# Small inputs as plain rows, and the output projection in longer runs, half of it loaded ahead of the last V tiles

## The chip, the cores and the metric

The kernel runs on one core of one Trainium2 chip. The metric is the device time in microseconds (us). All executions quoted here are fast (none is more than 1.5% above the fastest of its kernel), and their spread is given. A profiled execution is described by its span, from the first to the last instruction. The span is about 1.7 us shorter than the device time of the same execution.

A ratio below is the mean time of one kernel's fast runs over the mean time of the other's fast runs of the same rounds. It is therefore not quite the ratio of the medians that stand beside it. The interval is 95%. "Faster" and "slower" as verdicts need 2%.

## The reference

One decode step for four sequences (B = 4, one token each, D = 1024) mixes an attention block and an MLP block with a gate. H = 32 heads, Sk = 8192 cached positions, Dh = 128, F = 3584, all bf16. Cut to what matters:

```python
g = sigmoid((x * gate_w).sum(-1))
# A: attention over the cache
q = (x @ wq).reshape(B, 1, H, Dh)
p = softmax(q . k_cache * Dh**-0.5)
a = (p . v_cache).reshape(B, 1, H * Dh) @ wo
# B: MLP, scaled by sigmoid(x @ w_r)
y = (silu(x @ w_gate) * (x @ w_up)) @ w_down
b = x + y * sigmoid(x @ w_r)
return g * a + (1 - g) * b
```

The K and V caches are 268 MB each and each byte is used once. With the weights the kernel reads 576 MB.

## The kernel before

All large inputs go through a ring of five buffers of 128 x 32 KB (4 MB each), loaded by one queue (SP) in a fixed order. A "piece" is one such load: two heads of K or V of one sequence, or a part of a weight matrix. A piece is loaded as soon as the ring's oldest buffer has been used. There are 64 K pieces and 64 V pieces. V runs four pieces behind K, so the last four V pieces come after the last K. I call them V60 to V63.

The small inputs come in on another queue (ACT), already transposed by the access pattern, in runs of 16 bytes:

```python
    with nc.allow_non_contiguous_dma(reason="16-byte runs of x, w_r and gate_w"):
        nc.scalar.dma_start(out=xT[:], in_=x2.rearrange("b (c t) -> c b t", t=DT))
        nc.scalar.dma_start(out=wrg[:, 0, :], in_=B_w_r.rearrange("(c t) -> c t", t=DT))
        nc.scalar.dma_start(out=wrg[:, 1, :], in_=gate_w.rearrange("(c t) -> c t", t=DT))
    nc.scalar.dma_start(out=x_sb[:], in_=x2)
```

The program starts with the gates, which need `wrg` and `xT`, and then with q, which needs wq and `xT`:

```python
    gates()
    wq_piece(0)
    wq_piece(TW)
    q_done()
    # ... [cut: the list of MLP pieces put between the first K and V pieces]
    for u in range(NT + LAG):
        if u < NT:
            k_piece(u)
        if u >= LAG:
            v_piece(u - LAG)
        # ... [cut]
```

One V piece is 32 matmuls of 128x8 by 128x512, a copy by ScalarE, and four small fp32 matmuls that transpose the result back (the profile counts them as eight). After every fourth piece VectorE writes the normalized result of eight heads to `OT`:

```python
        o_sb = osp.tile([NM, 4 * Dh], F32, name="o_sb")
        nc.scalar.copy(out=o_sb[:], in_=o_ps[:])
        def finish():
            # ... [cut]
            for q in range(4):
                nc.tensor.matmul(oT[:, HT * t:HT * t + HT], lhsT=o_sb[:, q * Dh:(q + 1) * Dh],
                                 rhs=ident[0:NM, q:NM:4], start=(q == 0), stop=(q == 3))
            if t == GT - 1:
                # ... [cut: OT = oT * gate / row sum]
```

The output projection comes last, in pieces of 16, 12, 3 and 1 heads. Each run in memory is one row of wo, 2 KB:

```python
    wov = A_wo.rearrange("(h d) n -> d h n", d=P)
    def wo_piece(h0, nh):
        w = slot()[:, :nh * D].rearrange("p (h n) -> p h n", h=nh)
        nc.sync.dma_start(out=w, in_=wov[:, h0:h0 + nh, :])
        for h in range(nh):
            for n in range(NH):
                mm_acc(acc[:, n * NB:(n + 1) * NB], OT[:, h0 + h, :], w[:, h, n * NB:(n + 1) * NB])
```

Of the kernel before, what the change touches and what calls it, by code (L numbers as in the profile page):

```python
# [9 lines left out]
BF = mybir.dt.bfloat16  # L10
F32 = mybir.dt.float32
# [8 lines left out]
def kernel(  # L20
# [22 lines left out]
    nc = tc.nc  # L43
    P = 128
    Bn, Sq, D = A_x.shape
    _, H, Sk, Dh = A_k_cache.shape
    F = B_w_gate.shape[1]
    DT = D // P
# [4 lines left out]
    GH = GT * HT  # L53
# [3 lines left out]
    NT = Bn * H // HT  # L57
    LAG = 4
    FR = 4
    FG = F // (P * FR)  # L60
    NB = 512
    NH = D // NB
    RING = JR * Dh
# [3 lines left out]
    x2 = A_x.rearrange("b s d -> (b s) d")  # L67
    out2 = out.rearrange("b s d -> (b s) d")

    const = ctx.enter_context(tc.tile_pool(name="const", bufs=1))  # L70
# [8 lines left out]
    ops = ctx.enter_context(tc.tile_pool(name="ops", bufs=2, space=PSUM))  # L79
    o2p = ctx.enter_context(tc.tile_pool(name="o2p", bufs=1, space=PSUM))  # L80

    def slot():
        return ring.tile([P, RING], BF, name="piece", tag="piece")


    xT = const.tile([P, Bn, DT], BF)
    wrg = const.tile([P, 2, DT], BF)
    x_sb = const.tile([Bn, D], BF)
    with nc.allow_non_contiguous_dma(reason="16-byte runs of x, w_r and gate_w"):
        nc.scalar.dma_start(out=xT[:], in_=x2.rearrange("b (c t) -> c b t", t=DT))  # L90
        nc.scalar.dma_start(out=wrg[:, 0, :], in_=B_w_r.rearrange("(c t) -> c t", t=DT))
        nc.scalar.dma_start(out=wrg[:, 1, :], in_=gate_w.rearrange("(c t) -> c t", t=DT))
    nc.scalar.dma_start(out=x_sb[:], in_=x2)


    shr = shrp.tile([P, 512], F32)
    nc.vector.memset(shr[:], 0.0)
    ident = const.tile([P, P], F32)
    make_identity(nc, ident[:])
    R = const.tile([P, 4, P], BF)  # L100
    nc.gpsimd.memset(R[:], 0.0)
    for he in range(4):
# [21 lines left out]
    qT = const.tile([P, H, Bn], BF)  # L124
    qa = const.tile([P, 4, H, Bn], BF)
    OT = const.tile([P, H, Bn], BF)
    hT = const.tile([P, FG, FR, Bn], BF)
    sgb = const.tile([P, 2, Bn], F32)
    c12 = const.tile([P, 2, Bn], F32)
# [3 lines left out]
    gu_ps = shr[:, o0:o0 + 2 * FT * Bn].rearrange("p (w g r b) -> p w g r b", w=2, g=FG, r=FR); o0 += 2 * FT * Bn  # L133
# [3 lines left out]
    acc = accp.tile([Bn, D], F32)  # L137

    def mm_acc(out_ap, lhsT, rhs, start=False):
        nc.tensor.matmul(out_ap, lhsT=lhsT, rhs=rhs, start=start, stop=True, skip_group_check=True)  # L140


    def gates():
        wrep = ttp.tile([P, 2, DT, P], BF, name="wrep", tag="T")
        for i in range(2):
            nc.vector.tensor_copy(out=wrep[:, i, :, :], in_=wrg[:, i, :].unsqueeze(2).to_broadcast([P, DT, P]))  # L146
            for t in range(DT):
                mm_acc(rg_ps[:, i, :], wrep[:, i, t, :], xT[:, :, t])
        nc.scalar.activation(out=sgb[:], in_=rg_ps, func=ACT.Sigmoid)
        nc.vector.tensor_scalar(out=c12[:, 0, :], in0=sgb[:, 1, :], scalar1=-1.0, scalar2=1.0, op0=ALU.mult, op1=ALU.add)  # L150
        nc.vector.tensor_tensor(out=c12[:, 1, :], in0=c12[:, 0, :], in1=sgb[:, 0, :], op=ALU.mult)
        xf = ttp.tile([Bn, D], F32, name="xf", tag="T")
        nc.vector.tensor_copy(out=xf[:], in_=x_sb[:])
        dg = const.tile([Bn, Bn], F32)
        nc.vector.tensor_tensor(out=dg[:], in0=ident[0:Bn, 0:Bn], in1=c12[0:Bn, 0, :], op=ALU.mult)
        for n in range(NH):
            mm_acc(acc[:, n * NB:(n + 1) * NB], dg[:], xf[:, n * NB:(n + 1) * NB], start=True)
# [3 lines left out]
    wgv = B_w_gate.rearrange("(c t) f -> c t f", t=DT)  # L161
    wuv = B_w_up.rearrange("(c t) f -> c t f", t=DT)
    wdv = B_w_down.rearrange("(g f r) n -> f g r n", f=P, r=FR)
    wov = A_wo.rearrange("(h d) n -> d h n", d=P)
    TW = 4

    def wq_piece(t0):
        w = slot()[:, :TW * H * Dh].rearrange("p (t h d) -> p t h d", t=TW, h=H)
        nc.sync.dma_start(out=w.rearrange("p t h d -> p t (h d)"), in_=wqv[:, t0:t0 + TW, :])
        for t in range(TW):  # L170
            for h in range(H):
                mm_acc(q_ps[:, h, :], w[:, t, h, :], xT[:, :, t0 + t])

    def q_done():
        nc.vector.tensor_copy(out=qT[:], in_=q_ps)
# [6 lines left out]
    def gu_piece(view, w_i, t0):  # L182
        w = slot()[:, :TW * F].rearrange("p (t g f r) -> p t g f r", t=TW, g=FG, r=FR)
        nc.sync.dma_start(out=w.rearrange("p t g f r -> p t (g f r)"), in_=view[:, t0:t0 + TW, :])
        for t in range(TW):
            for g in range(FG):
                for r in range(FR):
                    mm_acc(gu_ps[:, w_i, g, r, :], w[:, t, g, :, r], xT[:, :, t0 + t])

    def h_done():  # L190
        g_sb = stat.tile([P, FT, Bn], F32, tag="g_sb", bufs=1)
        fl = lambda ap: ap.rearrange("p g r b -> p (g r) b")
        nc.scalar.activation(out=g_sb[:], in_=fl(gu_ps[:, 0]), func=ACT.Silu)
        nc.vector.tensor_tensor(out=g_sb[:], in0=g_sb[:], in1=fl(gu_ps[:, 1]), op=ALU.mult)
        nc.vector.tensor_tensor(out=fl(hT[:]), in0=g_sb[:],
                                in1=c12[:, 1:2, :].to_broadcast([P, FT, Bn]), op=ALU.mult)

    def wd_piece(g0, ng):
        w = slot()[:, :ng * FR * D].rearrange("p (g r n) -> p g r n", g=ng, r=FR)
        nc.sync.dma_start(out=w.rearrange("p g r n -> p g (r n)"),  # L200
                          in_=wdv[:, g0:g0 + ng].rearrange("f g r n -> f g (r n)"))
        for g in range(ng):
            for r in range(FR):
                for n in range(NH):
                    mm_acc(acc[:, n * NB:(n + 1) * NB], hT[:, g0 + g, r, :], w[:, g, r, n * NB:(n + 1) * NB])

    def wo_piece(h0, nh):
        w = slot()[:, :nh * D].rearrange("p (h n) -> p h n", h=nh)
        nc.sync.dma_start(out=w, in_=wov[:, h0:h0 + nh, :])
        for h in range(nh):  # L210
            for n in range(NH):
                mm_acc(acc[:, n * NB:(n + 1) * NB], OT[:, h0 + h, :], w[:, h, n * NB:(n + 1) * NB])


    S_ps = {}
# [4 lines left out]
    def flush():  # L220
        while pending:
            pending.pop(0)()
# [4 lines left out]
    def kv_view(cache, u):  # L227
        b, h0 = heads(u)
        return cache[b, h0:h0 + HT].rearrange("h (r j) d -> (h r) (j d)", j=JR)
# [63 lines left out]
    def v_piece(u):  # L293
        b, h0 = heads(u)
        g, t = divmod(u, GT)
        B_ = PB[g % 2]
        vn = slot()
        nc.sync.dma_start(out=vn[:], in_=kv_view(A_v_cache, u))
        o_ps = ops.tile([NM, 4 * Dh], F32, name="o_ps")
        n = 0  # L300
        for jc in range(JC):
            for uq in range(4):
                j0 = 16 * jc + 4 * uq
                nc.tensor.matmul(o_ps[:, :], lhsT=B_[:, JC * t + jc, uq].rearrange("p s j -> p (s j)"),  # L304
                                 rhs=vn[:, j0 * Dh:(j0 + 4) * Dh], start=(n == 0), stop=(n == JR // 4 - 1))
                n += 1
                if n == 8:
                    flush()
# [4 lines that stand above are left out]
            if t == 0:  # L313
                oT_t[g] = o2p.tile([P, GH], F32, name="oT")
            oT = oT_t[g]
# [4 lines that stand above are left out]
                oT_t.pop(g)  # L320
                hg = h0 + HT - GH
                nc.vector.scalar_tensor_tensor(out=OT[:, hg:hg + GH, b], in0=oT[:, :], scalar=sgb[:, 1, b:b + 1],  # L322
                                               in1=rinv_t.pop(g)[:], op0=ALU.mult, op1=ALU.mult)
        pending.append(finish)
# [5 lines left out]
    q_done()  # L330
    side = [lambda: gu_piece(wgv, 0, 0), lambda: gu_piece(wgv, 0, TW), lambda: gu_piece(wuv, 1, 0),
            lambda: (gu_piece(wuv, 1, TW), h_done()), lambda: wd_piece(0, 4), lambda: wd_piece(4, FG - 4)]
    for u in range(NT + LAG):
        if u < NT:
            k_piece(u)
        if u >= LAG:
            v_piece(u - LAG)
        if side:
            side.pop(0)()
    for s in side:  # L340
        s()
    flush()
    h0 = 0
    for nh in (16, 12, 3, 1):
        if h0 + nh <= H:
            wo_piece(h0, nh)
            h0 += nh
    assert h0 == H
    res = const.tile([Bn, D], BF)
    nc.vector.tensor_copy(out=res[:, 0:NB], in_=acc[:, 0:NB])  # L350
    nc.sync.dma_start(out=out2[:, 0:NB], in_=res[:, 0:NB])
# [32 lines left out]
```

## Time and profile before

| | before |
|---|---|
| device time, median of 4 runs | 1361.61 us (1361.4 to 1361.76) |
| span of the profiled run | 1359.9 us |
| bytes moved | 576.49 MB |
| first use of a wq piece | 48.4 us |
| first transpose of the last K piece | 1280.6 us |
| last output matmul ends | 1356.5 us |

The overview page has a line with the rate of the transfers in 40 equal slices of the span (34 us each), in GB/s:

```profile
GB/s 398 389 431 430 428 430 431 432 430 430 431 431 430 430 430 431 432 431 431 430 431 431 431 431 431 431 431 431 431 432 431 431 430 430 430 430 431 430 425 237
```

36 of the 40 slices are at 428 to 432. At 431 GB/s the bytes need 1337.5 us, and the span is 22 us longer. All of that is in the first two slices and the last two. As long as the middle stays at that rate, faster compute there cannot show in the time.

*The front.* The first lines of the chain of waits, in order of time (start in us, duration in us, what the time went to):

```profile
1.29 41.08 DMA wrg<-in_B_w_r_dram
42.37 0.02 issue
42.39 1.31 DVE wrep L146 x2
...
48.42 5.51 PE shr L140 x203
```

For 41 us TensorE and VectorE wait for w_r, a vector of 2 KB. The transfers run meanwhile, since the ring can be filled without anyone using it. But only four of its five buffers were being filled. SP, which issues these loads, waited 37.3 us for xT, one of the small inputs, before it issued the fifth:

```profile
40.05 0.33 SPq L242 DMA_DIRECT2D piece<-in_A_k_cache_dram  x1
```

For 41 us TensorE and VectorE wait for w_r, a vector of 2 KB. The ring can be filled meanwhile, but the sixth load needed a free buffer, so it had to wait until the first wq piece had been used (51.96 us). The transfers run dry. The windows show GB/s (the columns are the window and its length, busy us and number of instructions of PE, PE weight loads, DVE, ACT, POOL, then the granted TensorE clock, the DMA share and GB/s):

```profile
40.00:45.00 5.00, 0.91 (x17) 0.67 (x18) 2.45 (x9) 0.18 (x1) 0.00 (x0) 1.00 0.90 314
50.00:55.00 5.00, 4.82 (x182) 4.76 (x179) 0.00 (x0) 0.00 (x0) 0.00 (x0) 1.00 0.84 312
55.00:60.00 5.00, 1.62 (x30) 1.12 (x28) 3.63 (x4) 1.28 (x1) 1.56 (x8) 1.00 0.93 387
```

Against 431 GB/s this is a loss of 1.35 + 1.4 + 0.5 = 3.3 us. The queue table gives packets, MB, and share of the 16 engines' time; q1 is SP's queue, q10 is ACT's:

```profile
q1 hardware_dynamic: 24392, 575.68, 98.9%
q10 hardware_dynamic: 832, 0.02, 0.0%
```

So the small loads cost no DMA time to speak of, yet take 41 us to land. The same view for the stretch from 5 to 40 us shows why: in these 35 us both queues moved the same number of packets (469 of SP's have 28 or 32 KB, 501 of ACT's have 16 bytes, and the rest of both have 4 bytes).

```profile
q1 hardware_dynamic: 517, 14.86, 99.5%
q10 hardware_dynamic: 517, 0.01, 0.8%
```

*The tail.* The end of the chain of waits:

```profile
1292.97 7.01 PE o_ps L304 x32
...
1300.01 40.80 DMA piece<-in_A_wo_dram
...
1340.85 15.67 PE acc L140 x64
...
1356.55 0.57 ACT res L352
```

The long DMA link is the time in the queue of the first wo piece, behind the rest of V61, V62 and V63 (322 packets of 32 KB were still to come at 1300.0). TensorE's own list shows that it had to wait 1.91 us for V63.

```profile
1330.09 8.75 PE L304 MATMUL o_ps<-piece,PB_129 128*8 128x512 bf16 x32 [1.91 <-DMA piece<-in_A_v_cache_dram]
```

32 such matmuls take 7.07 us at full clock; here they took 8.75 us, with the clock granted in that window at 0.66. The Trainium skill ("TensorE: Matmul & The Clock Gate", Part 1) says that idleness halves TensorE's clock, in windows of 3.4 us; the trace agrees: its clock records have half clock from 1330.66 to 1334.07 us, and again from 1340.90 to 1344.31, where the 64 output matmuls took 15.67 us instead of 14.1 (twice 7.07).

### The profile page before, as it was taken

What the parts mean: (1) busy time and instruction counts of PE and PEld (TensorE: products, weight loads), DVE (VectorE), ACT (ScalarE), POOL (GpSimd) and SP (SyncE); (2) the same over time, 40 slices, a digit from 0 to 9 for tenths busy, and PEclk for the clock granted to TensorE, in tenths of its full rate; (3) what the DMA queues carried; (4) which work ended last, traced back from release to release, by engine and by line L of the source; (5) the groups of instructions that cost most, each with busy time, mean ns of one, the idle gap of its engine ahead of it and who ended that gap; (6) DMA issues with size and microseconds to landing.
All of it is one profiled execution on the core that took longest, in us unless ns stands there. A gap on an engine that the chain in (4) does not pass through costs nothing.

```text
span 1359.9 us, 12458 instructions
## 1 busy us (share of the span) xinstructions
PE 1115.9 (82%) x5456; PEld 481.1 (35%) x5456; DVE 621.3 (46%) x399; ACT 70.9 (5%) x118; POOL 84.2 (6%) x322
## 2 busy tenths in 40 slices
PE   0595998888888888878798888978988888888897
PEld 0352333333333333333333333333333333333343
DVE  0364355444544545365445535554554445445500
ACT  0000000000000000000000000000000000000010
POOL 1000000000000000000000000000000000000000
PEclk9987998999898989989999998989989998989998
DMA  9999999999999999999999999999999999999996
GB/s 398 389 431 430 428 430 431 432 430 430 431 431 430 430 430 431 432 431 431 430 431 431 431 431 431 431 431 431 431 432 431 431 430 430 430 430 431 430 425 237
DMA packets 25278, 576.49 MB, mean 424 GB/s; under 512 B 3068, under 2 KB 3076, under 8 KB 7176
## 3 DMA queue, kind: packets, MB, share of 16 engines
q1 hardware_dynamic: 24392, 575.68, 98.9%
q8 instruction: 42, 0.69, 0.2%
q10 hardware_dynamic: 832, 0.02, 0.0%
q14 instruction: 12, 0.10, 0.0%
HBM read 575.69 MB, written 0.01 MB: 423 GB/s over the span
## 4 chain that ended last, share of the span: by engine, by line
DMA 44%; PE 39%; DVE 11%; issue 4%; ACT 1%; POOL 0%; ACTq 0%; DVEq 0%
DMA piece<-in_A_k_cache_dram 38%; PE S_ps L252 17%; PE o_ps L304 17%; DVE T L245 11%; DMA wrg<-in_B_w_r_dram 3%; DMA piece<-in_A_wo_dram 3%; PE acc L140 2%; PE shr L140 2%; PE oT L317 1%; ACT o_sb L310 1%; DVE OT L322 0%; DVE wrep L146 0%; POOL PB_128 L282 0%; ACT PTs L275 0%; DVE PT L277 0%
## 5 line engine op out<-in xcount | busy, mean ns | idle before, releaser
L245 DVE STREAM_TRANSPOSE T<-piece 128x2048 uint32<-128x2048 uint32 x256 | 577.3, 2291 | 487.9 <-DMA piece<-in_A_k_cache_dram 390.0
L252 PE MATMUL S_ps<-T,Z_126 128*128 128x512 bf16 x1024 | 281.8, 429 | 92.9 <-DVE T L245 92.6
L252 PE MATMUL S_ps<-T,Z_127 128*128 128x512 bf16 x1024 | 264.0, 408 | 54.5 <-DVE T L245 54.5
L304 PE MATMUL o_ps<-piece,PB_129 128*8 128x512 bf16 x1024 | 227.9, 381 | 2.0 <-DMA piece<-in_A_v_cache_dram 1.9
L304 PE MATMUL o_ps<-piece,PB_128 128*8 128x512 bf16 x1024 | 226.2, 379 | 0.0
L252 PEld LDWEIGHTS <-Z_126 128*128 128x128 bf16 x1024 | 108.9, 106 | 253.2 <-issue 168.4
L252 PEld LDWEIGHTS <-Z_127 128*128 128x128 bf16 x1024 | 103.5, 102 | 201.3 <-issue 107.7
L304 PEld LDWEIGHTS <-PB_129 128*8 128x8 bf16 x1024 | 86.9, 87 | 139.0 <-issue 16.3
L304 PEld LDWEIGHTS <-PB_128 128*8 128x8 bf16 x1024 | 86.4, 87 | 137.3 <-issue 13.6
L317 PE MATMUL oT<-ident,o_sb 8*128 8x2 f32 x512 | 67.1, 249 | 46.3 <-ACT o_sb L310 46.3
L317 PEld LDWEIGHTS oT<-ident,o_sb 8*128 8x128 f32 x512 | 61.6, 186 | 78.5 <-ACT o_sb L310 78.5
L310 ACT COPY o_sb<-o_ps 8x512 f32<-8x512 f32 x64 | 36.7, 574 | 923.0 <-PE o_ps L304 923.0
L236 POOL COPY Z_126<-qa 32x4 bf16<-32x4 bf16 x128 | 24.9, 195 | 567.8 <-PE S_ps L252 523.0
L236 POOL COPY Z_127<-qa 32x4 bf16<-32x4 bf16 x128 | 24.9, 194 | 549.6 <-PE S_ps L252 544.1
L322 DVE SCALAR_TENSOR_TENSOR OT<-oT,sgb,rinv 128x8 bf16<-128x8 f32 x16 | 3.8, 236 | 89.9 <-PE oT L317 89.9
L140 PE MATMUL shr<-xT,wrep 128*128 128x4 bf16 x16 | 0.8, 171 | 43.4 <-DVE wrep L146 43.4
L140 PEld LDWEIGHTS <-piece 128*128 128x128 bf16 x704 | 22.5, 112 | 2.9 <-issue 2.0
L140 PE MATMUL shr<-xT,piece 128*128 128x4 bf16 x704 | 22.6, 171 | 0.2 <-issue 0.2
L275 ACT ACTIVATE PTs<-S_ps,negm 128x512 bf16<-128x512 f32 x16 | 11.0, 687 | 224.0 <-DVE negm L272 224.0
L146 DVE COPY wrep<-wrg 128x1024 bf16<-128x1024 bf16 x2 | 1.3, 690 | 40.9 <-DMA wrg<-in_B_w_r_dram 40.9
L277 DVE STREAM_TRANSPOSE PT<-PTs 128x512 bf16<-128x512 bf16 x16 | 11.4, 712 | 13.5 <-ACT PTs L275 13.5
L140 PEld LDWEIGHTS <-wrep 128*128 128x128 bf16 x16 | 0.6, 106 | 43.4 <-DVE wrep L146 43.4
(85 smaller groups left out, 133.7 us busy)
## 6 DMA issues: line engine op xcount, KB each, us to landing
piece<-in_A_k_cache_dram SPq DMA_DIRECT2D x64, 4096.0 KB, 38.0
piece<-in_A_v_cache_dram SPq DMA_DIRECT2D x64, 4096.0 KB, 37.9
piece<-in_A_wq_dram SPq DMA_DIRECT2D x2, 4096.0 KB, 22.6
piece<-in_B_w_gate_dram SPq DMA_DIRECT2D x2, 3584.0 KB, 40.0
piece<-in_B_w_up_dram SPq DMA_DIRECT2D x2, 3584.0 KB, 17.3
piece<-in_B_w_down_dram SPq DMA_DIRECT2D x1, 4096.0 KB
piece<-in_A_wo_dram SPq DMA_DIRECT2D x1, 4096.0 KB
piece<-in_B_w_down_dram SPq DMA_DIRECT2D x1, 3072.0 KB, 24.3
```

The costliest lines, as they stand in the source:

```text
L140: nc.tensor.matmul(out_ap, lhsT=lhsT, rhs=rhs, start=start, stop=True, skip_group_check=True)
L146: nc.vector.tensor_copy(out=wrep[:, i, :, :], in_=wrg[:, i, :].unsqueeze(2).to_broadcast([P, DT, P]))
L236: nc.gpsimd.tensor_copy(out=Z[32 * a:32 * a + 32, :, 31 + 32 * a:32 + 32 * a], in_=qa[32 * a:32 * a + 32, :, h0 + a // QH, b:b + 1])
L245: nc.vector.transpose(out=T[:].rearrange("p j h i e -> p (j h i e)").bitcast(U32), in_=kn[:, c * CJ * Dh:(c + 1) * CJ * Dh].bitcast(U32))
L252: nc.tensor.matmul(sps[:, :], lhsT=Z[:, he, s:s + P], rhs=T[:, 16 * jl:16 * jl + 16, half, :, e], start=(t == 0 and jc == 0 and he == 0), ...
L275: nc.scalar.activation(out=PTs[:], in_=sps[:], func=ACT.Exp, bias=negm[:, 0:1], scale=scale, accum_out=rs[:, 0:1])
L277: nc.vector.transpose(out=PT[:].rearrange("p j i -> p (j i)"), in_=PTs[:])
L304: nc.tensor.matmul(o_ps[:, :], lhsT=B_[:, JC * t + jc, uq].rearrange("p s j -> p (s j)"), rhs=vn[:, j0 * Dh:(j0 + 4) * Dh], start=(n == 0) ...
L310: nc.scalar.copy(out=o_sb[:], in_=o_ps[:])
L317: nc.tensor.matmul(oT[:, HT * t:HT * t + HT], lhsT=o_sb[:, q * Dh:(q + 1) * Dh], rhs=ident[0:NM, q:NM:4], start=(q == 0), stop=(q == 3))
L322: nc.vector.scalar_tensor_tensor(out=OT[:, hg:hg + GH, b], in0=oT[:, :], scalar=sgb[:, 1, b:b + 1], in1=rinv_t.pop(g)[:], op0=ALU.mult, op ...
```

## The change

The intent at the front is to load x, w_r and gate_w as six plain rows of 2 KB and to transpose them on TensorE. The intent at the tail is threefold. wo is read in runs of 8 KB (four consecutive rows per partition), which makes it necessary to permute the attention output the same way (`o_rows`, 16 small matmuls with a strided identity). The first 4 MB of wo are loaded ahead of V61 and used before it. The last V comes in four transfers of 1 MB. The core of the diff:

```diff
-        nc.scalar.dma_start(out=xT[:], in_=x2.rearrange("b (c t) -> c b t", t=DT))
-        nc.scalar.dma_start(out=wrg[:, 0, :], in_=B_w_r.rearrange("(c t) -> c t", t=DT))
-        nc.scalar.dma_start(out=wrg[:, 1, :], in_=gate_w.rearrange("(c t) -> c t", t=DT))
-    nc.scalar.dma_start(out=x_sb[:], in_=x2)
+    x6 = const.tile([NX, D], BF)
+    nc.scalar.dma_start(out=x6[0:Bn], in_=x2)
+    nc.scalar.dma_start(out=x6[Bn:Bn + 1], in_=B_w_r.rearrange("(o n) -> o n", o=1))
+    nc.scalar.dma_start(out=x6[Bn + 1:Bn + 2], in_=gate_w.rearrange("(o n) -> o n", o=1))
 # ... [cut]
+    for t in range(DT):
+        nc.tensor.transpose(out=xw_ps[:, t, :], in_=x6[:, t:D:DT], identity=identb[0:NX, 0:NX])
 # ... [cut: uses of xT; and below, o_rows]
-    wov = A_wo.rearrange("(h d) n -> d h n", d=P)
+    wov = A_wo.rearrange("(g p r) n -> p g r n", p=P, r=FR)
+    def wo_piece(g0, g1, r0=0, r1=FR):
+        ng, nr = g1 - g0, r1 - r0
+        w = slot()[:, :ng * nr * D].rearrange("p (g r n) -> p g r n", g=ng, r=nr)
+        nc.sync.dma_start(out=w.rearrange("p g r n -> p g (r n)"),
+                          in_=wov[:, g0:g1, r0:r1].rearrange("p g r n -> p g (r n)"))
 # ... [cut: returns a function that does the matmuls, on LT instead of OT]
-        nc.sync.dma_start(out=vn[:], in_=kv_view(A_v_cache, u))
+        cut = 4 if u == NT - 1 else 1
+        for c in range(cut):
+            lo, hi = c * RING // cut, (c + 1) * RING // cut
+            nc.sync.dma_start(out=vn[:, lo:hi], in_=vv[:, lo:hi])
 # ... [cut]
+    GE = NWB - GH // WB          # 6 of 8 groups of 512 rows
+    GS = GE // 2 + 1             # 4
     for u in range(NT + LAG):
         if u < NT:
             k_piece(u)
+        if u == NT + 1:
+            flush()
+            o_rows(0, GE)
+            wo_piece(0, GS)()
         if u >= LAG:
             v_piece(u - LAG)
-    for nh in (16, 12, 3, 1):
-        # ... [cut]
+    early = wo_piece(GS, GE)
+    late = [wo_piece(GE, NWB - 1), wo_piece(NWB - 1, NWB, 0, FR - 1), wo_piece(NWB - 1, NWB, FR - 1, FR)]
     flush()
+    early()
+    o_rows(GE, NWB)
+    for use in late:
+        use()
```

More of the change, by code (lines that the diff above doesn't have):

```diff
@@ L83, in slot @@
         return ring.tile([P, RING], BF, name="piece", tag="piece")
-    xT = const.tile([P, Bn, DT], BF)
-    wrg = const.tile([P, 2, DT], BF)
-    x_sb = const.tile([Bn, D], BF)
-    with nc.allow_non_contiguous_dma(reason="16-byte runs of x, w_r and gate_w"):
-        nc.scalar.dma_start(out=xT[:], in_=x2.rearrange("b (c t) -> c b t", t=DT))
-        nc.scalar.dma_start(out=wrg[:, 0, :], in_=B_w_r.rearrange("(c t) -> c t", t=DT))
-        nc.scalar.dma_start(out=wrg[:, 1, :], in_=gate_w.rearrange("(c t) -> c t", t=DT))
-    nc.scalar.dma_start(out=x_sb[:], in_=x2)
+    NX = Bn + 2
+    x6 = const.tile([NX, D], BF)
+    nc.scalar.dma_start(out=x6[0:Bn], in_=x2)
+    nc.scalar.dma_start(out=x6[Bn:Bn + 1], in_=B_w_r.rearrange("(o n) -> o n", o=1))
+    nc.scalar.dma_start(out=x6[Bn + 1:Bn + 2], in_=gate_w.rearrange("(o n) -> o n", o=1))
     shr = shrp.tile([P, 512], F32)
@@ L99 @@
     make_identity(nc, ident[:])
+    identb = const.tile([P, P], BF)
+    nc.vector.tensor_copy(out=identb[:], in_=ident[:])
+    xw_ps = o2p.tile([P, DT, NX], BF, name="xw", tag="oT")
+    for t in range(DT):
+        nc.tensor.transpose(out=xw_ps[:, t, :], in_=x6[:, t:D:DT], identity=identb[0:NX, 0:NX])
+    xw = const.tile([P, DT, NX], BF)
+    nc.vector.tensor_copy(out=xw[:], in_=xw_ps[:])
+    xT = [xw[:, t, 0:Bn] for t in range(DT)]
     R = const.tile([P, 4, P], BF)
@@ L126 @@
     OT = const.tile([P, H, Bn], BF)
+    LT = const.tile([P, FR, H // FR, Bn], BF)
     hT = const.tile([P, FG, FR, Bn], BF)
@@ L145, in gates @@
         for i in range(2):
-            nc.vector.tensor_copy(out=wrep[:, i, :, :], in_=wrg[:, i, :].unsqueeze(2).to_broadcast([P, DT, P]))
+            nc.vector.tensor_copy(out=wrep[:, i, :, :], in_=xw[:, :, Bn + i:Bn + i + 1].to_broadcast([P, DT, P]))
             for t in range(DT):
-                mm_acc(rg_ps[:, i, :], wrep[:, i, t, :], xT[:, :, t])
+                mm_acc(rg_ps[:, i, :], wrep[:, i, t, :], xT[t])
         nc.scalar.activation(out=sgb[:], in_=rg_ps, func=ACT.Sigmoid)
@@ L152, in gates @@
         xf = ttp.tile([Bn, D], F32, name="xf", tag="T")
-        nc.vector.tensor_copy(out=xf[:], in_=x_sb[:])
+        nc.vector.tensor_copy(out=xf[:], in_=x6[0:Bn])
         dg = const.tile([Bn, Bn], F32)
@@ L171, in wq_piece @@
             for h in range(H):
-                mm_acc(q_ps[:, h, :], w[:, t, h, :], xT[:, :, t0 + t])
+                mm_acc(q_ps[:, h, :], w[:, t, h, :], xT[t0 + t])
     def q_done():
@@ L187, in gu_piece @@
                 for r in range(FR):
-                    mm_acc(gu_ps[:, w_i, g, r, :], w[:, t, g, :, r], xT[:, :, t0 + t])
+                    mm_acc(gu_ps[:, w_i, g, r, :], w[:, t, g, :, r], xT[t0 + t])
     def h_done():
@@ L205, in wd_piece, with o_rows, use @@
                     mm_acc(acc[:, n * NB:(n + 1) * NB], hT[:, g0 + g, r, :], w[:, g, r, n * NB:(n + 1) * NB])
-    def wo_piece(h0, nh):
-        w = slot()[:, :nh * D].rearrange("p (h n) -> p h n", h=nh)
-        nc.sync.dma_start(out=w, in_=wov[:, h0:h0 + nh, :])
-        for h in range(nh):
-            for n in range(NH):
-                mm_acc(acc[:, n * NB:(n + 1) * NB], OT[:, h0 + h, :], w[:, h, n * NB:(n + 1) * NB])
+    WB = P * FR // Dh
+    NWB = H // WB
+    def o_rows(g0, g1):
+        n = g1 - g0
+        lp = ops.tile([P, FR, n, Bn], F32, name="o_ps")
+        for k in range(WB):
+            for r in range(FR):
+                nc.tensor.matmul(lp[32 * k:32 * k + 32, r], lhsT=identb[:, r:P:FR],
+                                 rhs=OT[:, WB * g0 + k:WB * g1:WB, :], start=True, stop=True, skip_group_check=True)
+        nc.vector.tensor_copy(out=LT[:, :, g0:g1, :], in_=lp[:])
+    def wo_piece(g0, g1, r0=0, r1=FR):
[3 more added lines that the diff above has]
+                          in_=wov[:, g0:g1, r0:r1].rearrange("p g r n -> p g (r n)"))
+        def use():
+            for g in range(ng):
+                for r in range(nr):
+                    for n in range(NH):
+                        mm_acc(acc[:, n * NB:(n + 1) * NB], LT[:, r0 + r, g0 + g, :], w[:, g, r, n * NB:(n + 1) * NB])
+        return use
     S_ps = {}
@@ L297, in v_piece @@
         vn = slot()
-        nc.sync.dma_start(out=vn[:], in_=kv_view(A_v_cache, u))
+        vv = kv_view(A_v_cache, u)
+        cut = 4 if u == NT - 1 else 1
+        for c in range(cut):
+            lo, hi = c * RING // cut, (c + 1) * RING // cut
+            nc.sync.dma_start(out=vn[:, lo:hi], in_=vv[:, lo:hi])
         o_ps = ops.tile([NM, 4 * Dh], F32, name="o_ps")
@@ L339 @@
             side.pop(0)()
-    for s in side:
-        s()
+    early = wo_piece(GS, GE)
+    late = [wo_piece(GE, NWB - 1), wo_piece(NWB - 1, NWB, 0, FR - 1), wo_piece(NWB - 1, NWB, FR - 1, FR)]
     flush()
-    h0 = 0
-    for nh in (16, 12, 3, 1):
-        if h0 + nh <= H:
-            wo_piece(h0, nh)
-            h0 += nh
-    assert h0 == H
+    early()
+    o_rows(GE, NWB)
+    for use in late:
+        use()
     res = const.tile([Bn, D], BF)
```

## The prediction

> **What bounds the kernel now.** The transfers. The 40-slice page shows 428 to 432 GB/s in 36 of 40 slices; 576.49 MB at 431 GB/s is 1337.5 us of a 1359.9 us span, so 22 us are lost, at the two ends. The groups agree: VectorE waits 390 us for K pieces.
>
> *Front.* The chain starts with 41.1 us of DMA for w_r. TensorE cannot use wq until x and w_r are there, so none of the ring's five 4 MB slots comes free. The windows show 314 GB/s in 40:45, 312 in 50:55, 387 in 55:60: against 431 a loss of 1.35 + 1.4 + 0.5 = 3.3 us. The queue table gives the cause: 832 packets on the ACT queue, 0.0% of the engines' time, yet 41 us. The Trainium skill ("DMA: Bandwidth & Descriptors", Queues, rings and completion order) says each DMA engine alternates between queue rows packet by packet; 16-byte packets behind 28 to 32 KB ones fit that.
>
> *Tail.* The last V lands near 1330 (TensorE idles 1.9 us for it), its matmuls end at 1338.9, the transpose back at 1340.6, 64 output matmuls take 15.7 us to 1356.5; copy, store and end 3.4 us. The last wo transfer is done by 1351: TensorE ends this stage.
>
> **The change.** Front: 6 rows of 2 KB replace 768 16-byte runs; they should land within 10 us. Added: an identity cast, 8 small transposes, one copy. The identity is only ready at 13.9 us (timeline), so wq is used from about 16 us instead of 48, before the ring drains at 47: the 3.3 us stall goes, plus perhaps 0.2 us of packet cost. Gain 3.5 us, all critical, carried through the DMA-bound middle: last K at 1277 instead of 1280.5.
>
> Tail: half of wo (4 MB, 9.7 us) moves ahead of V61. DMA lands, at 9.73 us per 4 MB: V59 1286.5, V60 1296, wo 1306, V61 1316, V62 1325.5, V63 1335 in quarters, rest of wo by 1345. From V62's landing TensorE has 7.07 (V62) + 1.05 (transpose back) + 7.07 (V63) + 0.65 (ScalarE copy) + 1.05 + 0.35 (OT), 16 permuting matmuls (estimate 1.2), 32 output matmuls at 0.22 (7.1): 25.5 us, end 1351. So it is TensorE-bound from V62 on. Before, V63's landing to the last matmul took 26.5 us; now 16 plus the 9.7 of wo put in front: about 1 us gained. The 8 KB runs save 1 us per 4 MB (10.7 against 9.7), but where nothing waits any more.
>
> Clock: the windows show 0.66 granted in 1330:1335 and 1340:1345, after idle stretches. "TensorE: Matmul & The Clock Gate" (Part 1) says idleness halves the clock in 3.4 us windows; each costs some 1.8 us here. The new tail may have one too.
>
> **Prediction.** Last matmul 1351, +3.4 = 1354.4 span, +1.7 from span to time = 1356.1, plus 0.9 for half a throttle window: 1357.0 us, 8 in 10 between 1353 and 1360. Faster by over 2% 0.01, within 2% 0.98, slower 0.01.
>
> **Signs.** Right: no 41 us DMA link at the start; slices 1 and 2 near 430 after the first 3 us; first output matmuls near 1307; the final chain TensorE from V62 or V63 on, late wo landed before use. Wrong: a new DMA dip before 60 us; the last wo piece as last releaser; V61 to V63 waiting for slots.
>
> **What would make it wrong.** Small rows landing late after all; output or permuting matmuls slower than 0.22 and 0.08 us; throttle windows falling differently; the early wo making TensorE late at V61.

## The result, and the profile after

| | before | changed |
|---|---|---|
| device time, median of 4 runs | 1361.61 us (1361.4 to 1361.76) | 1357.22 us (1356.14 to 1358.29) |
| ratio of the fast runs | | 0.9968 (0.9951 to 0.9985) |
| span of the profiled run | 1359.9 us | 1354.7 us |
| first use of a wq piece | 48.4 us | 23.5 us |
| first transpose of the last K piece | 1280.6 us | 1276.6 us |
| last output matmul ends | 1356.5 us | 1351.7 us |

The changed kernel is 4.4 us faster by the medians, 0.3%. The spans differ by 5.2 us, because the profiled run was one of the two quicker of the four. Of these 5.2 us, 4.0 were there when the last K piece was transposed. Only 0.8 us were gained from there to the last output matmul, and 0.4 us behind it. Counted in the packet records of the two traces, any number of bytes between 22 and 545 MB was reached about 3.5 us earlier (3.1 to 3.8) in the changed kernel. Some 1.3 to 1.75 us of that are there at 17 to 20 MB, in the fifth load, and the rest comes with the sixth.

The rates of the slices, page of the changed kernel. The second slice went from 389 to 428; the middle is as it was:

```profile
GB/s 404 428 432 427 427 432 430 433 431 429 430 431 430 433 431 430 429 432 431 430 433 431 430 431 430 429 432 432 431 433 431 432 428 429 431 432 433 432 422 257
```

ACT's queue in the queue table has 20 packets instead of 832:

```profile
q10 hardware_dynamic: 20, 0.02, 0.0%
```

SP issues the fifth load at 2.84 us instead of 40.05. The front of the chain of waits no longer has a DMA link. It begins with 11.54 us in which POOL waited for nothing that the profile shows, and then POOL builds constants, among them the identity (13.56 us in the kernel before, so this is not new, only hidden no longer). Then follow a VectorE cast of 2.12 us (0.67 in the kernel before; why, was not looked into), the fp32 matmuls of the residual, and the first use of wq at 23.57 us:

```profile
1.73 11.54 issue
13.27 0.28 POOL ident masks.py:199
...
17.34 2.12 DVE xf L159
...
20.00 3.57 PE acc L146 x4
23.57 5.29 PE shr L146 x195
```

The windows in which the transfers had run dry (the same columns as before) now show 455, 392 and 454 GB/s:

```profile
40.00:45.00 5.00, 4.25 (x19) 1.77 (x18) 4.39 (x2) 0.00 (x0) 0.00 (x0) 1.00 1.05 455
50.00:55.00 5.00, 0.51 (x4) 0.18 (x2) 2.83 (x2) 0.00 (x0) 0.00 (x0) 0.54 0.92 392
55.00:60.00 5.00, 4.46 (x16) 1.66 (x15) 3.92 (x3) 0.00 (x0) 0.00 (x0) 0.78 1.05 454
```

The mean of the three is 434, and the slice that holds them (34 to 68 us) is at 428 instead of 389, so the 392 is at most a small part of the old loss. The end of the chain of waits:

```profile
1275.09 42.07 DMA piece<-in_A_v_cache_dram
1317.16 0.04 issue
1317.20 8.51 PE o_ps L333 x32
...
1326.42 1.05 PE oT L346 x8
1327.47 8.73 PE o_ps L333 x40
1336.19 0.98 PE oT L346 x8
1337.17 5.29 PE o_ps L333 x24
...
1343.16 1.06 PE oT L346 x8
...
1344.25 0.25 DVE OT L351
...
1344.88 6.87 PE acc L146 x31
```

From V61's landing at 1317.16 us there is no DMA in the chain any more. TensorE works through V61, V62 and V63 (32 + 40 + 24 matmuls; the 40 are V62 and the first quarter of V63), the transposes back, and the last 32 output matmuls. TensorE's own list shows the price of the early piece ahead of V61:

```profile
1307.48 7.07 PE L146 MATMUL acc<-piece,LT 128*4 128x512 bf16 x32 [0.99 <-DMA piece<-in_A_wo_dram]
1317.20 8.50 PE L333 MATMUL o_ps<-piece,PB_139 128*8 128x512 bf16 x32 [2.65 <-DMA piece<-in_A_v_cache_dram]
```

It takes TensorE 7.07 us to use 4 MB of wo, and the transfers 9.7 us to bring them. The difference is a wait of 2.65 us before V61, and the clock then is halved for a part of V61 (8.50 instead of 7.07 us).

### The profile page after: what moved, and what is told of

It reads as the page before. It is cut to its first block, busy times and chain, and to the rows that moved or that the text cites. A ratio compares the mean times of both kernels' runs of the same rounds, so it can differ in the third digit from the quotient of the medians.

```text
span 1354.7 us, 12547 instructions
## 1 busy us (share of the span) xinstructions
PE 1119.6 (83%) x5496; PEld 483.1 (36%) x5496; DVE 624.2 (46%) x403; ACT 71.0 (5%) x118; POOL 85.2 (6%) x322
## 4 chain that ended last, share of the span: by engine, by line
DMA 48%; PE 33%; DVE 11%; issue 7%; ACT 1%; POOL 0%; DVEq 0%; ACTq 0%; POOLq 0%
DMA piece<-in_A_k_cache_dram 45%; PE o_ps L333 17%; PE S_ps L277 13%; DVE T L270 10%; DMA piece<-in_A_v_cache_dram 3%; PE acc L146 1%; PE oT L346 1%; PE shr L146 1%; ACT o_sb L339 1%; DVE OT L351 0%; DVE xf L159 0%; POOL Z_137 L127 0%; POOL R L109 0%; POOL PB_138 L307 0%; DVEq L270 0%
## 5 line engine op out<-in xcount | busy, mean ns | idle before, releaser
L333 PEld LDWEIGHTS <-PB_138 128*8 128x8 bf16 x1024 | 86.4, 87 | 137.3 <-issue 13.6
L146 PE MATMUL shr<-xw,piece 128*128 128x4 bf16 x704 | 22.6, 170 | 1.7 <-issue 1.7
L146 PE MATMUL acc<-piece,LT 128*4 128x512 bf16 x64 | 14.1, 379 | 1.0 <-DMA piece<-in_A_wo_dram 1.0
L313 DVE RECIPROCAL rinv<-tot 128x8 f32<-128x8 f32 x16 | 3.2, 203 | 25.3 <-POOL tot L311 25.3
L146 PE MATMUL acc<-piece,hT 128*4 128x512 bf16 x56 | 12.4, 379 | 0.0
## 6 DMA issues: line engine op xcount, KB each, us to landing
piece<-in_A_wq_dram SPq DMA_DIRECT2D x2, 4096.0 KB, 13.1
```

What stands on the lines that cost most here:

```text
L146: nc.tensor.matmul(out_ap, lhsT=lhsT, rhs=rhs, start=start, stop=True, skip_group_check=True)
L313: nc.vector.reciprocal(out=rinv[:], in_=tot[:])
L333: nc.tensor.matmul(o_ps[:, :], lhsT=B_[:, JC * t + jc, uq].rearrange("p s j -> p (s j)"), rhs=vn[:, j0 * Dh:(j0 + 4) * Dh], start=(n == 0) ...
```

## The experiments

Theory A: the front brings the gain, because in a kernel bound by transfers a stall of the transfers is never made up; in the tail TensorE has a fixed sum of work behind the last V pieces, and neither run length nor the early half removes any of it. Theory B: the tail brings the gain. (The expectations also name a theory C or D, or a rival, for a single run.) Twelve kernels ran, all correct, each for five rounds beside the kernel before. The medians of before in the three groups of runs were 1361.32, 1361.60 and 1361.65 us.

| run | median us (range) | ratio to before (95%) |
|---|---|---|
| front_only | 1357.32 (1356.93 to 1358.68) | 0.9973 (0.9960 to 0.9985) |
| tail_only | 1361.97 (1360.47 to 1363.41) | 1.0006 (0.9994 to 1.0019) |
| wo_all_late | 1357.68 (1356.81 to 1358.17) | 0.9973 (0.9961 to 0.9986) |
| small_behind_wq | 1357.61 (1357.61 to 1359.41) | 0.9977 (0.9963 to 0.9991) |
| no_cut | 1357.60 (1356.91 to 1358.55) | 0.9970 (0.9956 to 0.9984) |
| more_early | 1358.46 (1358.38 to 1361.22) | 0.9983 (0.9970 to 0.9995) |
| late_split | 1352.66 (1352.46 to 1353.31) | 0.9933 (0.9921 to 0.9946) |
| keep_warm | 1357.43 (1355.67 to 1357.77) | 0.9964 (0.9951 to 0.9976) |
| late_split_2k | 1353.99 (1353.80 to 1354.32) | 0.9941 (0.9929 to 0.9954) |
| simple_both | 1354.61 (1354.52 to 1354.74) | 0.9945 (0.9933 to 0.9958) |
| keep_warm_2 | 1357.31 (1355.66 to 1357.94) | 0.9962 (0.9950 to 0.9975) |
| after_again | 1357.69 (1355.76 to 1359.12) | 0.9967 (0.9953 to 0.9980) |

### front_only: the front alone

Edit: the changed kernel with the old tail put back.

```diff
-    wov = A_wo.rearrange("(g p r) n -> p g r n", p=P, r=FR)
+    wov = A_wo.rearrange("(h d) n -> d h n", d=P)
 # ... o_rows, early half and the cut of the last V removed; 16, 12, 3, 1 heads at the end
```

Expected:

> The new loads of x, w_r and gate_w with the old tail (2 KB runs of wo, all of it after the last V, last V in one transfer). Theory A, front first: the ended stall moves every later transfer 3.5 to 3.9 us forward and the old tail follows unchanged, so 1357.9 us (1357.3 to 1358.5), last K in the trace near 1276.7 instead of 1280.5. Theory B, tail first: a stall in the first 60 us is made up in the 1250 us that follow, or the old tail waits for something else, and this kernel stays above 1360.5 us.

Measured: 1357.32 us, 4.0 us below before by the medians. The last K landed at 1276.5 us in the chain of waits. Theory A holds for the front, and within the spread this is all of the gain of the full change (1357.22 and, again, 1357.69 us).

### tail_only: the tail alone

Edit: the kernel before with the new tail (and the bf16 identity that it needs).

```diff
+    identb = const.tile([P, P], BF)
+    nc.vector.tensor_copy(out=identb[:], in_=ident[:])
-    wov = A_wo.rearrange("(h d) n -> d h n", d=P)
+    wov = A_wo.rearrange("(g p r) n -> p g r n", p=P, r=FR)
 # ... o_rows, early half and the cut of the last V as in the change
```

Expected:

> The old loads with the new tail. Theory A: last K as before at 1280.5 us, the tail from there on shorter by 0.5 to 2 us, so 1360.6 us (1359.6 to 1361.3). Theory B, the early half of wo and its 8 KB runs bring most of the gain: 1358.5 us or less.

Measured: 1361.97 us, ratio 1.0006 with an interval from 0.9994 to 1.0019. The gain of about 1 us that theory A gave it did not appear (the median is 0.7 us above A's range), and the gain of 3 us that theory B gave it is excluded. In the profiled run two half-clock stretches fell into the tail: 40 matmuls of V took 10.13 us instead of 8.8, and the last 31 output matmuls 8.55 instead of 6.87. They don't explain the missing gain, for the tail of the kernel before has two as well. Without them, the old tail took 26.5 - 3.2 = 23.3 us from V63's landing (1330.05) to the last output matmul, and the new one 27.4 - 3.0 = 24.4 us from V62's landing at nearly the same time (1330.30). At equal clock the new tail is no shorter.

### small_behind_wq: old 16-byte runs, other queue

Edit, against the kernel before: the four small loads are issued on the queue of the weights, directly behind the first wq piece.

```diff
+    wq0 = slot()[:, :4 * H * Dh].rearrange("p (t h d) -> p t h d", t=4, h=H)
+    nc.sync.dma_start(out=wq0.rearrange("p t h d -> p t (h d)"),
+                      in_=A_wq.rearrange("(c t) n -> c t n", t=DT)[:, 0:4, :])
-        nc.scalar.dma_start(out=xT[:], in_=x2.rearrange("b (c t) -> c b t", t=DT))
+        nc.sync.dma_start(out=xT[:], in_=x2.rearrange("b (c t) -> c b t", t=DT))
 # ... the same for w_r, gate_w and x_sb; wq_piece(0) uses wq0
```

Expected:

> The kernel before, 16-byte runs kept, but the four small loads are issued on the same queue as the weights, directly behind the first wq piece. Theory A (each small packet had to let a 28 to 32 KB packet of the other queue pass): on one queue they run one after the other and land at 12 to 16 us instead of 41, and the time is 1358.2 us (1357.5 to 1358.9), as with plain rows. Rival C (the 16-byte runs are slow in themselves): w_r lands after 25 us or later, or the transfers behind them are held up by as much, and at least 1360.5 us.

Measured: 1357.61 us. The list of DMA issues (queue, count, KB, us from issue to landing) of the kernel before:

```profile
wrg<-in_B_w_r_dram ACTq DMA_DIRECT2D x1, 2.0 KB, 41.1
wrg<-in_gate_w_dram ACTq DMA_DIRECT2D x1, 2.0 KB, 40.7
```

and of small_behind_wq:

```profile
wrg<-in_B_w_r_dram SPq DMA_DIRECT2D x1, 2.0 KB, 13.1
wrg<-in_gate_w_dram SPq DMA_DIRECT2D x1, 2.0 KB, 12.7
```

The same 16-byte runs land in 13.1 us, most of which is the 4 MB of wq ahead of them: in the packet records all 768 start between 12.0 and 14.1 us. Rival C, that the short runs are slow in themselves, falls. The 41 us came from standing in a queue of their own beside a queue of large packets. The Trainium skill ("DMA: Bandwidth & Descriptors", Queues, rings and completion order) says that each DMA engine takes turns between the queues that have work, one packet at a time. The trace of the kernel before agrees: 517 packets of each queue from 5 to 40 us, so a turn cost a small packet 1.08 us (35 us on 16 engines for 517 packets). The plain rows and the transposes of the change are therefore one cure of two, and the other one needs no new instruction.

### wo_all_late: nothing of wo ahead of a V

Edit, against the changed kernel:

```diff
-            wo_piece(0, GS)()
-    early = wo_piece(GS, GE)
+    early = [wo_piece(0, GS), wo_piece(GS, GE)]
 # ... and both are used behind the last V
```

Expected:

> The changed kernel, but the first 4 MB of wo are loaded after the last V, with the same 8 KB runs; nothing of wo stands ahead of a V. Theory A: TensorE's work after the last K is the same and only its waits move (about 3 us for the first wo piece instead of 3.7 us before V61), so the last output matmul ends near 1350 to 1351.5 in the trace and the time is 1355 to 1357.5 us, no slower than the changed kernel. Theory B: half the output matmuls go back behind the last V, 32 times 0.22 us, so 1361 us or more.

Measured: 1357.68 us, 0.2 us above the range given, and the same as the changed kernel (1357.22 and 1357.69). Moving half of wo ahead of V61 is worth nothing that can be measured: theory B does not hold. Theory A's time was nearly met, but not its trace, where the last output matmul was to end by 1351.5 us; in the profiled run it ended at 1353.3. TensorE's list shows what it waits for now:

```profile
1336.67 16.65 PE L146 MATMUL acc<-piece,LT 128*4 128x512 bf16 x64 [2.51 <-DMA piece<-in_A_wo_dram]
```

It waits 2.51 us for the first wo piece of 4 MB, and then runs 64 matmuls in 16.65 us, at half clock for a part of them, where 64 at full clock take 14.1 (2 x 7.07).

### late_split: the same in transfers of 1 MB

Edit, against wo_all_late:

```diff
-        nc.sync.dma_start(out=w.rearrange("p g r n -> p g (r n)"),
-                          in_=wov[:, g0:g1, r0:r1].rearrange("p g r n -> p g (r n)"))
+        for g in range(ng):
+            nc.sync.dma_start(out=w[:, g].rearrange("p r n -> p (r n)"),
+                              in_=wov[:, g0 + g, r0:r1].rearrange("p r n -> p (r n)"))
```

Expected:

> All of wo behind the last V as in the run with wo all late, but in transfers of 1 MB (one group of 512 rows) instead of 4 and 2 MB. Theory A: the first group lands some 7 us earlier, so the 2.5 us wait of TensorE for the first wo piece goes and the half-clock window behind it with it; TensorE then follows the transfers, whose end was near 1346.3: last matmul 1346.8 to 1348, time 1351.7 to 1353.5 us. Rival (TensorE's sum of work fixes the end wherever the waits are): 1356 us or more.

Measured: 1352.66 us, ratio 0.9933 (0.9921 to 0.9946). This is 9 us below before and 4.6 to 5 us below the changed kernel. TensorE's list from the last V on:

```profile
1326.35 5.34 PE L334 MATMUL o_ps<-piece,PB 128*8 128x512 bf16 x24
1331.53 1.03 PE L146 MATMUL acc<-piece,LT 128*4 128x512 bf16 x4
1332.49 1.05 PE L347 MATMUL oT<-ident,o_sb 8*128 8x2 f32 x8
...
1341.76 1.89 PE L146 MATMUL acc<-piece,LT 128*4 128x512 bf16 x8 [0.24 <-DMA piece<-in_A_wo_dram]
1344.24 3.76 PE L146 MATMUL acc<-piece,LT 128*4 128x512 bf16 x16 [0.60 <-DMA piece<-in_A_wo_dram]
```

The first output matmuls run at 1331.5, in the very gap in which the last V's result is copied by ScalarE. In wo_all_late they started at 1336.7. No half-clock stretch follows (there is none between 1281.6 us and the last matmul), and at the end TensorE waits for transfers (0.24 and 0.60 us) instead of the other way round. The chain of waits ends with a wo transfer, and the last 16 matmuls end at 1348.0. The rival, that TensorE's sum of work fixes the end wherever its waits are, falls, and with it the tail half of theory A: what was too long was not the sum, but the waits in it. The two items that went, the wait of 2.51 us and the 2.5 us that half clock cost the 64 matmuls in wo_all_late, make up the 5.0 us between the two medians. The time also spreads less, 0.9 us between the fastest and the slowest run against 2 to 3 us for the changed kernel.

### more_early: 6 MB of wo ahead of V61

Edit, against the changed kernel:

```diff
             wo_piece(0, GS)()
+            wo_piece(GS, GE)()
-    early = wo_piece(GS, GE)
-    early()
```

Expected:

> The changed kernel with 6 MB of wo ahead of V61 instead of 4 MB; 2 MB remain behind the last V. Theory A: V61 to V63 land 4.9 us later, in which TensorE does the 16 extra output matmuls (3.5 us), and 16 matmuls fewer stand behind the last V: last matmul near 1349.5, 1355 us (1353.5 to 1356.5). Theory D (the transfers end the stage, not TensorE): the same as the changed kernel, 1356.5 to 1357.7.

Measured: 1358.46 us, so this expectation was wrong by 3.5 us, and theory D was nearer. It is not D's mechanism, though, for the chain has no DMA behind V61:

```profile
1321.87 8.75 PE L333 MATMUL o_ps<-piece,PB 128*8 128x512 bf16 x32 [3.74 <-DMA piece<-in_A_v_cache_dram]
1332.32 8.80 PE L333 MATMUL o_ps<-piece,PB 128*8 128x512 bf16 x40
```

V61 landed at 1321.8, 4.7 us later than in the changed kernel (4.9 expected). My error was to take the 3.5 us off the end and to add nothing for the later V61. From V61's landing TensorE needs some 30 us even at full clock: three V pieces of 7.07 us, about 6 us of copies, transposes back and permutation between them, and 3.6 us of output matmuls. In the trace it took 31.9 us, with a half-clock stretch in V61. Two MB more ahead of V61 cost 4.7 us before V61 and save 3.5 us behind it. That makes 1.2 us of loss; by the medians it is 0.8 to 1.2 us, but the ranges of the two kernels overlap. So a larger early load doesn't help; that it harms is likely, not shown.

### no_cut: the last V in one transfer

Edit, against the changed kernel:

```diff
-        cut = 4 if u == NT - 1 else 1
+        cut = 1
```

Expected:

> The changed kernel with the last V in one 4 MB transfer instead of four. In the trace of the changed kernel its first 8 matmuls start near 1334.4 us, while the whole V should land near 1336.2 (the V before ended its transfer at 1326.4, plus 9.8). Theory A (TensorE-bound from V61 on): TensorE then waits some 1.8 us there and everything behind it moves by as much, 1358.5 to 1360 us. If the cut is worth nothing: 1356.5 to 1357.7 us.

Measured: 1357.60 us, the same as the changed kernel. It met the second of the two expectations, that the cut is worth nothing. The first, a wait of 1.8 us, fails: the profile shows no wait for the last V at all. The early output matmuls and V62 had a half-clock stretch each in that run (8.75 and 8.76 us instead of 7.07), and so kept TensorE busy until 1337.2, when the whole V63 was there. In the changed kernel the cut is worth nothing that can be measured. In the split kernels it was not tested alone.

### keep_warm and keep_warm_2: filling TensorE's wait

Edit, against the changed kernel: 12 matmuls whose result is not used, behind the early output matmuls. In the second version they read the early wo piece:

```diff
-            wo_piece(0, GS)()
+            wo_piece(0, GS, warm=12)()
 # ... in wo_piece, behind its matmuls:
+                for i in range(warm):
+                    nc.tensor.matmul(wp[0:Bn, :], lhsT=LT[:, r1 - 1, g1 - 1, :], rhs=w[:, ng - 1, nr - 1, D - NB:D],
+                                     start=(i == 0), stop=(i == warm - 1))
```

Expected:

> The changed kernel with 12 matmuls of 128x4 by 128x512 on constants, their result unused, behind the 32 early output matmuls: they fill the 2.65 us in which TensorE waits for V61. If the half clock in V61's matmuls (8.5 us for 32 instead of 7.07) comes from that wait, they run at 7.1 us and the time falls by about 1.4 us, to 1355.2 to 1356.2 us. If the half clock falls by chance, or the wait is not its cause, the time stays at 1356.5 to 1358.

> Keep_warm once more, the 12 unused matmuls now reading the early wo piece, so that they stand in TensorE's order between the early output matmuls and V61 (checked in the built kernel). If TensorE's wait for V61 causes the half clock in V61's matmuls, no half-clock window starts between 1310 and 1320 us and the median falls to 1355.2 to 1356.2 us. If not, it stays at 1356.5 to 1358.

Measured: the first version says nothing. Its matmuls depend on nothing loaded late, so they were put far ahead in TensorE's order and ran between 1227 and 1242 us. It is a changed kernel with 12 idle matmuls elsewhere: 1357.43 us. In the second version they stand where they should:

```profile
1314.14 2.75 PE L240 MATMUL S_ps<-piece,LT 128*4 128x512 bf16 x12
1316.96 7.07 PE L338 MATMUL o_ps<-piece,PB 128*8 128x512 bf16 x32
...
1326.71 10.33 PE L338 MATMUL o_ps<-piece,PB 128*8 128x512 bf16 x40 [0.92 <-DMA piece<-in_A_v_cache_dram]
```

V61 runs at full clock, 7.07 us. But a half-clock stretch comes 10 us later, in V62 (10.33 us instead of 8.8), and the median stays at 1357.31. The wait of 2.65 us is thus not the only thing that brings on the half clock.

What does can be counted in the clock records of the kept traces. In all 14 of them half clock comes in pieces of 3.41 us, or a multiple, on a fixed grid of such windows. From 1290 us to the last matmul, 18 half-clock windows follow one of full clock. In the window before each of them, the large matmuls (all but the fp32 ones that transpose back) filled at most 0.41 of the time. Before the 192 full-clock windows that follow one of full clock, they filled 0.41 or more. So in this tail it matters whether a single window of the grid catches most of a wait. In the changed kernel the window before V61 (1313.3 to 1316.7 us) was filled to 0.36, and half clock followed. keep_warm waited 2.12 us there too, but the wait lay across two windows, filled to 0.79 and 0.59, and V61 ran at full clock. Where the grid lies against the program differs from trace to trace. This is a count made afterwards; no run was made to test it.

### after_again: the spread of the changed kernel

No edit.

> The changed kernel unchanged, for the spread of its time beside these runs: 1356.1 to 1358.3 us as before, median near 1357.2.

Measured: 1357.69 us, from 1355.76 to 1359.12. The profiled run (1357.79 us) had two half-clock stretches in the tail, one in the early output matmuls and one in V62. The windows' third column from the right is the granted clock:

```profile
1307.00:1311.00 4.00, 3.56 (x10) 1.07 (x9) 0.00 (x0) 0.00 (x0) 0.00 (x0) 0.57 1.01 434
1327.00:1331.00 4.00, 4.00 (x12) 1.28 (x13) 0.00 (x0) 0.00 (x0) 0.00 (x0) 0.60 1.00 418
```

The first profiled run of the changed kernel (1356.53 us) had one there, and keep_warm's (1355.67 us) had none behind V60. So the range of some 2 to 3 us fits the number and place of these stretches, each of which costs 1.3 to 1.7 us of TensorE's time. That it is fully explained by them was not tested, since only profiled runs show them.

### late_split_2k and simple_both: is the rest of the change needed?

late_split_2k is front_only with the last V cut in four and wo in transfers of 1 MB, but in the old 2 KB runs, without the permutation. simple_both does the same to small_behind_wq, so it is the kernel before with nothing changed but how loads are issued. The edit of the tail, the same in both:

```diff
-        nc.sync.dma_start(out=w, in_=wov[:, h0:h0 + nh, :])
+        for h in range(0, nh, 4):
+            n = min(4, nh - h)
+            nc.sync.dma_start(out=w[:, h:h + n, :], in_=wov[:, h0 + h:h0 + h + n, :])
```

Expected:

> The new loads, the last V in four transfers, all of wo behind it in 1 MB transfers, but with the 2 KB runs of the kernel before and no permuted attention output. Theory A: with 1 MB transfers the end of the loads decides, and the last load ended at 1347.4 us with 2 KB runs (front only) against 1346.3 with 8 KB runs, so 1 to 2 us slower than late_split: 1353.7 us (1353 to 1355). If the run length is worth nothing: 1352.4 to 1353.0. If it is what made late_split fast: 1356 us or more.

> The kernel before with three edits of issue order and size only: small loads behind the first wq piece on the same queue, last V in four transfers, wo in 1 MB transfers with 2 KB runs. No transposes, no permutation. Theory A: the front gain of small_behind_wq and the tail gain of late_split_2k add, 1353.9 us (1353 to 1355.3). If the plain rows or the permutation matter beyond that: 1356 us or more.

Measured: 1353.99 and 1354.61 us, both within their ranges. The runs of 8 KB, with the permutation that they need, are worth 1.3 us (1353.99 against 1352.66, from two groups of runs) once the transfers decide the end. Three edits of issue order and size give 7 of the 9 us, with no transposes and no permutation.

The version that beats both kernels is late_split, 1352.66 us: the change with its early half taken back and wo in 1 MB transfers.

## Why the prediction was right

The predicted time was 1357.0 us in a range of 1353 to 1360. Measured were 1357.22 us, and 1357.69 in the repeat. That the middle of the range was hit so closely is in part luck: the front gave 4.0 us instead of 3.5, and the tail nothing instead of 1. Point by point:

- *The front stall of 3.3 us goes, gain 3.5 us, carried unchanged to the last K: right.* The last K moved from 1280.6 to 1276.6 (predicted 1277), and front_only alone measured 4.0 us by the medians. In bytes moved the transfers were 3.5 us ahead; the other 0.5 us at the last K was not traced. The cause, packets of the small queue taking turns with large ones, was shown by small_behind_wq and by the packet counts. One link was missed: the prediction let the ring drain only at 47 us, with five buffers filled. The transfers ran dry at 40 us already, since SP itself waited for xT before it issued the fifth load.
- *wq is used from about 16 us: wrong by 7.5 us, without effect.* It was 23.5 us. The chain shows the POOL constants until 17.2, a VectorE cast of 2.1 us and 3.6 us of fp32 matmuls, which the estimate left out. The slack to 47 us, where five filled buffers run dry by the prediction's estimate, absorbed it.
- *The small rows land within 10 us: about right.* The last packet started at 11.1 us, and the first instruction that reads the rows at 11.6 us; the identity at 13.6 us was later and decided.
- *The tail gains about 1 us: the mis-sized term.* It measured nothing. The profiled run gained 0.8 us between the last K and the last output matmul, but it had one half-clock stretch there against two in the kernel before, and tail_only came out at a ratio of 1.0006 (0.9994 to 1.0019). The step that failed is the comparison of 25.5 us with 26.5: the 26.5 us were measured and hold two half-clock stretches (some 3.2 us), while the 25.5 us were summed at full clock, with 0.9 us for half a stretch added later. At equal clock the new tail is no shorter (24.4 against 23.3 us, see tail_only). The terms of the sum were mostly right: first output matmuls at 1307.5 (predicted 1307), last one ending at 1351.7 (predicted 1351). But the permutation took 0.33 us for 16 matmuls and not 1.2. V61 landed 1.2 us later than counted, and the half-clock stretches that I booked with 0.9 us came once in one profiled run and twice in the other.
- *TensorE-bound from V62 on: right, and one piece earlier.* The last DMA in the chain was V61. Late wo was there before it was used.
- *8 KB runs save transfer time where nothing waits any more: consistent in the changed kernel, and shown by contrast.* They became worth 1.3 us only in late_split, where transfers decide the end.

What the prediction did not see is that the tail could be 5 us shorter. It called the tail "TensorE-bound" and summed the work. The sum holds waits: 2.65 us before V61, the copies and transposes between V pieces, the half clock after them. late_split removed the wait for a 4 MB piece by smaller transfers and put the first output matmuls into the gap behind the last V.

## What to carry to other kernels

A small load that gates the start should not stand in a second queue beside a queue full of large packets. Put it on the same queue behind the first large piece, or make it a few long rows; a stall of the transfers early in this transfer-bound kernel was paid in full at the end. In the tail, where the compute engine ends the stage, loading the last weights ahead of the last data can help only if the engine has at least as much work on them as they take to arrive. Here they took 9.7 us to load and 7.07 us to use, and the difference became a wait. Smaller transfers in the old order gained 5 us where the reordering gained none.

## What the Trainium skill lacked or had wrong

- "DMA: Bandwidth & Descriptors", Issuing engines are not separate DMA queues, says that issuing from several engines "will only save the time on the sequencer it takes to initiate the DMA". Here it also sets the order of service: the same 16-byte runs landed after 41.1 us from a queue of their own and after 13.1 us behind the first wq piece on the queue of the weights.
- The same page, Queues, rings and completion order, states the turn-taking without a price. Here one turn of a 16-byte packet beside packets of 28 to 32 KB came to 1.08 us (517 packets of each queue on 16 engines in 35 us).
- "TensorE: Matmul & The Clock Gate", Part 1, ties the half clock to at least one idle window of about 3.4 us. Here the window need not be idle: half clock followed windows of 3.41 us that large matmuls had filled up to 0.41 of the time (18 cases in the tails of 14 traces), and no full-clock window with less than 0.41 was followed by full clock. A wait of 2.65 us was enough when it fell into one window.
